# Sums of values four pieces to a visit, and planned steps that keep GpSimd's subtractions from VectorE's sums

## Chip, cores and metric

The kernel runs on one core of a Trainium2 chip. The metric is the device time of one execution in microseconds (us); lower is better. Before the change the median of three runs is 1843.38 us (1842.33 to 1844.65).

## What is computed

Agent attention over 4 batches of 12480 tokens of width 128 with 49 agents, and a two-layer network with a squared ReLU on its result. Cut to what matters:

```python
def sm(a, b):                                  # batches B = 4
    s = scale * (a @ b.transpose(0, 2, 1))     # scale = 1 / sqrt(128)
    s = s - s.max(-1, keepdims=True)
    e = np.exp(s)
    return e / (e.sum(-1, keepdims=True) + 1e-09)

a2k = sm(agents, k)          # 49 x 12480 for each batch
agent_v = a2k @ v            # 49 x 128
q2a = sm(q, agents)          # 12480 x 49
x = (q2a @ agent_v).reshape(49920, 128)
h = x @ w_in                 # 128 -> 2048
r = np.maximum(h, 0.0)
out = ((r * r) @ w_out).astype(np.float32)     # 2048 -> 128
```

All inputs are float32. The kernel splits both operands of each large product into a high and a low part and adds three products of the parts.

## The kernel before, in words

**The main loop.** The tokens are cut into 49 slabs of 1024. For each slab there are 16 steps (`NF`), for each tile of 512 tokens 8 steps (`NJ`), 784 in all. In step i, `mm1(i)` makes 256 hidden columns of one tile: six matmuls from the normalised query weights (`p_a`, `p_b`, high and low parts) and the folded weights `w_hi`, `w_lo`, which hold agent_v times w_in of the batch. ScalarE then takes the ReLU (`relu`), and for each two steps squares (`square`, 128x2048); VectorE makes the rounded high part `gh` (`high`, L453) and the low part `gl` (`low`, L457) of the square. `mm2` of step i works on the hidden columns of five steps earlier (`LAG`): twelve matmuls into one of two pairs of PSUM banks (`pair`), the last four from `gl`. After eight steps a tile is done; `store` adds the pair's two halves (ScalarE copy L482, VectorE sum `ob` L483) and sends the tile out.

**What is put between the steps.** TensorE, VectorE, ScalarE, GpSimd and the DMA queue of SyncE (SP) each execute their instructions in the order in which they are written out. That order comes from a list of (time in steps, function), which a planner fills and which is sorted at the end (`at`, `steps`). Every 16 steps the query path of one slab runs: for two slabs at a time `q_scores` on TensorE and `q_shift` on VectorE, then for each slab `q_exp` (ScalarE), `q_inverse` (VectorE), `q_norm` (GpSimd, L349), `q_hi` (ScalarE), `q_lo` (GpSimd, L362), a DMA transpose and sort, and the weave of two 16-bit planes (`q_weave`, half on ScalarE, half on GpSimd, L392), then `q_spread` by DMA into `p_a` and `p_b`.

**The next batch.** While batch b-1 is in the main loop, `plan_batch(b)` lays out the work on the keys and values of batch b = 1, 2, 3. Batch 0 is done ahead of the loop. The 12480 keys are 13 pieces of 960. First the key scores, two pieces to a visit of TensorE (`k_scores`, L179), with a copy to SBUF (`k_copy`) and a running maximum (`k_pmax`). When the maximum is known, each piece n gets `k_sub` (GpSimd, L214: the maximum is subtracted in place in `sk`), `k_exp` (ScalarE) and `e_sum` (VectorE, L232: the exponentials are added into `ea`). `v_acc` (TensorE, L229) multiplies the exponentials of some pieces with their values, 64 small matmuls a piece (128 records a visit of two pieces, as each fp32 matmul leaves two), in one visit between two steps of the main loop; `v_sum` (VectorE, L245, L247) adds its result to the sum of the batch. `v_load` fetches a piece of values into one of the nine buffers that key, query and value pieces and two stages of the query path share (`io`). At the batch's end `a_last` and `w_make_all` fold the result into `w_hi` and `w_lo`.

**The planner.** `chain(t, todo)` gives each operation of a list (engine, function, arguments) a whole step at or after t. `hop` holds the steps from one engine's operation to the next one's. A step that is in `taken` for an engine isn't given twice, with one exception: a VectorE operation that reads a bank directly behind its TensorE visit goes there all the same, and its step is put in `read`. Visits may only lie in steps in which the tile of `mm2` is at step 1, 3 or 5 (`slots`). The steps that carry a `store` are taken for ScalarE and VectorE (`ends`). The query path is planned first, then the batches. `low` has its place within a step by `read` and `ends`, so that moved visits move it by a fraction of a step. The planned steps set the order of instructions on each engine and nothing else: an engine executes its next instruction as soon as the inputs are there.

Of the kernel before, what the change touches and what calls it, by code (L numbers as in the profile page):

```python
# [25 lines left out]
def agent_attention_relu2_kernel(ctx: ExitStack, tc: tile.TileContext, qT, kT, v, agT, w_in, w_out, outT):  # L26
# [7 lines left out]
    B, NS = kT.shape[:2]  # L34
# [455 lines left out]
    def at(t, f, *args):  # L490
        steps.append((t, len(steps), f, args))
# [7 lines left out]
    slots = {i for i, m in second.items() if m % NJ in (1, 3, 5)}  # L499
    taken = {(e, i) for i in ends for e in ("ACT", "DVE")}  # L500
    read = set()

    def chain(t, todo):

        first = prev = None
        while todo:
            n = 1
            while todo[0][0] == "PE" and n < len(todo) and todo[n][1] in reads_bank and todo[n][0] != "PE":  # L510
                n += 1
            t += hop[prev][todo[0][0]] if prev else 0
            while True:
                g, p, ts = t, None, []
                for e, *_ in todo[:n]:
                    g += hop[p][e] if p else 0
                    while (e, g) in taken or (e == "PE" and g not in slots):
                        if p == "PE" and e == "DVE":
                            break
                        g += 1  # L520
                    ts.append(g)
                    p = e
                if todo[0][0] != "PE" or ts[-1] <= ts[0] + 1:
                    break
                t += 1
            for (e, f, *args), g in zip(todo, ts):
                soon = e == "DVE" and prev == "PE"
                if soon:
                    read.add(g)
                else:  # L530
                    taken.add((e, g))
                at(g + (.49 if soon and f is q_shift else .47 if soon else .45 if e == "PE" else .5), f, *args)
                prev = e
            first = ts[0] if first is None else first
            t, todo = ts[-1], todo[n:]
        return first, t
# [3 lines left out]
    def plan_tokens(s, base):  # L540
        todo = [("ACT", q_exp, s), ("DVE", q_inverse, s), ("POOL", q_norm, s), ("ACT", q_hi, s)]
        todo += [("POOL", q_lo, s)] + ([("PE", q_transpose, s), ("ACT", q_copy, s)] if s < 3 else [])
        if s > 1 and s % 2 == 0:
            m = min(2, NSG - s)
            first, base = chain(base, [("PE", q_scores, s, m), ("DVE", q_shift, s, m)])
            for x in range(s, s + m):
                at(first - 5, q_load, x)
            base += 3
        _, end = chain(base, todo)
        if s > 2:  # L550
            at(end + 2.4, q_turn, s)
            at(end + 4.9, q_sort, s)
            end += 8
            while any(("ACT", end + x) in taken for x in range(4)):
                end += 1
            _, end = chain(end, [("ACT", q_weave, s, 1, nc.scalar.copy)])
            taken.update(("ACT", end + x) for x in (1, 2))
            at(end + .6, q_weave, s, 0, nc.gpsimd.tensor_copy)
        at(max(end + 1.4, (s - 1) * NF + 9.9 if s % 2 else 0) if s > 2 else end + .9, q_spread, s)
        assert end + 3 < s * NF, (s, end)  # L560

    def plan_batch(b, base):

        end = b * N // TT * NJ
        for n in range(0, NS, 2):
            m = min(2, NS - n)
            first, t = chain(base + int(n * 4.6), [("PE", k_scores, b, n, m), ("ACT", k_copy, n, m), ("DVE", k_pmax, n, m)])
            for x in range(n, n + m):
                if b > 1 or x:
                    at(max(base - (6 if b > 1 else 0), first - 5), k_load, b, x)  # L570
            if n == NS - 3:
                chain(t + 1, [("DVE", k_max, 0, NS - 1)])
        _, t0 = chain(t + 1, [("DVE", k_max, 1)])
        _, t0 = chain(t0 + 4, [("PE", k_max, 2), ("DVE", k_max, 3)])
        _, t0 = chain(t0 + 3, [("PE", k_max, 4), ("DVE", k_max, 5)])
        done, d = {}, (end - 31 - t0) / NS
        for n in range(NS):
            _, done[n] = chain(t0 + 1 + int(n * d), [("POOL", k_sub, n), ("ACT", k_exp, n)])
            if n:
                _, y = chain(done[n] + 1, [("DVE", e_sum, n)])  # L580
            if n == NS - 1:
                _, y = chain(y + 1, [("DVE", a_last, 0)])
            if n % 2 or n == NS - 1:
                x = n - n % 2
                first, t = chain(done[n] + 2 if n % 2 else y + 4, [("PE", v_acc, x, n + 1 - x), ("DVE", v_sum, x)])
                for y in range(x, n + 1):
                    at(first - 5, v_load, b, y)
        at(first + .46, a_last, 1)
        at(t + .475, a_last, 2)
        _, e = chain(t + 2, [("PE", w_make_all, b, 0), ("ACT", w_make_all, b, 1), ("DVE", w_make_all, b, 2)])  # L590
        assert e + 2 < end, (e, end)
        return t + 1
# [30 lines left out]
    for n in range(NS):  # L623
        t = Z + 6.3 + 2.07 * n
# [43 lines left out]
    t = t0 + 13.4  # L668
# [22 lines left out]
    for y, x in enumerate((1.15, 1.16, 1.17)):  # L691
        at(x, w_first, 0, 4, 4, y, nc.vector)
    at(3.1, warm_rows, 6)
    plan_tokens(1, 3)
    for s in range(2, NSG):
        plan_tokens(s, (s - 2) * NF + (13 if s < 3 else 7 if s % 2 else 6))
    t = 0
    for b in range(1, B):
        t = plan_batch(b, t)
# [43 lines left out]
```

## Time and profile before

| | before |
|---|---|
| median of three runs | 1843.38 us |
| the profiled execution | 1842.06 us, its span 1840.3 us |
| TensorE busy | 1823.0 us, 99% |
| VectorE busy | 1689.1 us, 92% |
| ScalarE busy | 1676.8 us, 91% |
| GpSimd busy | 375.9 us, 20% |
| matmuls of the value visits (L229) | 2496 records in 21 visits |
| `k_sub` on GpSimd (L214) | 39 x 2238 ns |
| `e_sum` on VectorE (L232) | 33 x 879 ns and 3 x 1066 ns |

How to read it: the span runs from the first to the last instruction of the profiled execution; the rest of its time lies around it. Busy time is the sum of an engine's instructions. Matmuls overlap, so a busy TensorE isn't one at its peak; idle time in front of an instruction is shown with what ended it ("releaser").

### The profile page before, as it was taken

To read this page: it belongs to the slowest core of one execution; us is meant where nothing else is said; L and a number is where in the kernel's file an instruction comes from. 1 tells how busy PE (TensorE), PEld (TensorE's weight loads), DVE (VectorE), ACT (ScalarE), POOL (GpSimd) and SP (SyncE) were. 2 spreads that over 40 slices of the span, in tenths; PEclk is the share of its full clock that TensorE was granted. 3 is DMA by queue.
4 is the path that set the end of the run, shared out by engine and by line. 5 is a ranking of instruction groups with operands and counts; after the bars stand their busy time and mean duration, and the time that the engine had idled before them with its cause. 6 is when DMAs were issued, how large, how long until landed. Compare 5 with 4: busy or idle time off the path is not lost.

```text
span 1840.3 us, 51937 instructions
## 1 busy us (share of the span) xinstructions
PE 1823.0 (99%) x23244; PEld 1481.4 (80%) x23244; DVE 1689.1 (92%) x1274; ACT 1676.8 (91%) x1538; POOL 375.9 (20%) x199
## 2 busy tenths in 40 slices
PE   9899999999999999999999999999999999999999
PEld 8688888887888887878788788788878888888887
DVE  7789999999888999999988999999999999999997
ACT  5788999998989999999898999999999999999998
POOL 1111132222111222223111132132211112212110
PEclk9999999999999999999999999999999999999999
DMA  9334334434443334333434243324422322322320
GB/s 383 113 99 133 99 94 114 110 101 120 111 121 118 89 106 113 86 109 91 135 113 130 77 97 100 119 80 115 119 64 86 87 74 80 92 74 80 81 74 21
DMA packets 154514, 193.46 MB, mean 105 GB/s; under 512 B 102488, under 2 KB 102744, under 8 KB 154290
## 3 DMA queue, kind: packets, MB, share of 16 engines
q1 hardware_dynamic: 154290, 190.13, 35.5%
q8 instruction: 182, 2.98, 0.7%
q14 instruction: 42, 0.34, 0.1%
HBM read 83.02 MB, written 25.56 MB: 59 GB/s over the span
## 4 chain that ended last, share of the span: by engine, by line
PE 86%; ACT 5%; DVE 4%; issue 2%; DMA 1%; POOL 0%; SPq 0%; ACTq 0%; DVEq 0%; POOLq 0%
PE pair L477 53%; PE h L440 27%; PE pair L179 3%; ACT rg L446 3%; ACT rg L449 2%; PE pair L229 2%; DVE gl L457 2%; DVE gh L453 1%; DMA raw<-w_in 1%; PE pair L238 1%; DMA p_b<-w_lo 0%; PE pair L298 0%; POOL e L349 0%; ACT ob L482 0%; DVE e L334 0%
## 5 line engine op out<-in xcount | busy, mean ns | idle before, releaser
L457 DVE TENSOR_TENSOR gl<-rg,gh 128x2048 fp32r<-128x2048 f32 x391 | 937.6, 2398 | 18.6 <-DVE gh L453 0.9
L446 ACT ACTIVATE rg<-h 128x1024 f32<-128x1024 f32 (+1 forms) x784 | 790.9, 1020 | 118.7 <-PE h L440 116.6
L449 ACT ACTIVATE rg<-rg 128x2048 f32<-128x2048 f32 x391 | 748.7, 1915 | 7.3
L477 PE MATMUL pair<-gh,wo_hi 64*128 64x512 f32 x3136 | 632.3, 391 | 1.4 <-issue 1.4
L477 PE MATMUL pair<-gh,wo_lo 64*128 64x512 f32 x3136 | 633.4, 392 | 0.0
L453 DVE CAST gh<-rg 128x2048 fp32r<-128x2048 f32 x391 | 520.1, 1330 | 90.9 <-ACT rg L449 80.7
L477 PE MATMUL pair<-gl,wo_hi 64*128 64x512 f32 x3136 | 501.1, 391 | 4.0 <-DVE gl L457 3.1
L440 PE MATMUL h<-p_b,w_hi 49*128 49x512 f32 (+4 forms) x1616 | 503.2, 390 | 1.8 <-DMA p_b<-w_lo 1.8
L440 PE MATMUL h<-p_a,w_hi 49*128 49x512 f32 (+4 forms) x1616 | 498.3, 390 | 1.3 <-ACT rg L446 0.6
L477 PEld LDWEIGHTS pair<-gh,wo_lo 64*128 64x128 f32 x3136 | 314.6, 186 | 70.8 <-issue 2.2
L477 PEld LDWEIGHTS pair<-gh,wo_hi 64*128 64x128 f32 x3136 | 312.4, 185 | 66.7
L477 PEld LDWEIGHTS pair<-gl,wo_hi 64*128 64x128 f32 x3136 | 303.7, 184 | 72.0 <-DVE gl L457 5.4
L440 PEld LDWEIGHTS h<-p_a,w_hi 49*128 49x128 f32 x1616 | 287.6, 186 | 43.7 <-issue 3.2
L440 PEld LDWEIGHTS h<-p_b,w_hi 49*128 49x128 f32 x1616 | 290.9, 186 | 29.7 <-DMA p_b<-w_lo 2.4
L440 PE MATMUL h<-p_b,w_lo 49*128 49x512 f32 (+4 forms) x808 | 313.6, 388 | 0.0
L440 PE MATMUL h<-p_a,w_lo 49*128 49x512 f32 (+4 forms) x808 | 313.6, 388 | 0.0
L349 POOL TENSOR_TENSOR e<-e,sm 128x392 f32<-128x392 f32 x48 | 76.4, 1591 | 735.8 <-DVE sm L346 698.0
L392 POOL COPY woven<-planes 128x1024 uint16<-128x1024 uint16 x46 | 100.3, 2181 | 458.6 <-DMA planes<-turned 405.1
L440 PEld LDWEIGHTS h<-p_a,w_lo 49*128 49x128 f32 x808 | 148.4, 184 | 27.6
L440 PEld LDWEIGHTS h<-p_b,w_lo 49*128 49x128 f32 x808 | 148.4, 184 | 2.3
L362 POOL TENSOR_TENSOR pp<-e,pp 128x392 fp32r<-128x392 f32 x48 | 105.4, 2197 | 142.9 <-ACT pp L359 142.9
L214 POOL TENSOR_TENSOR sk<-sk,mM 120x392 f32<-120x392 f32 x39 | 87.2, 2238 | 15.6 <-DVE mM L211 15.6
(112 smaller groups left out, 854.8 us busy)
## 6 DMA issues: line engine op xcount, KB each, us to landing
vt<-v SPq DMA_DIRECT2D x52, 516.0 KB
qt<-qT SPq DMA_DIRECT2D x49, 512.0 KB
kt<-kT SPq DMA_DIRECT2D x52, 480.0 KB
outT<-ob SPq DMA_DIRECT2D x97, 256.0 KB
planes<-turned SPq DMA_DIRECT2D x184, 98.0 KB
p_a<-woven SPq DMA_DIRECT2D x92, 196.0 KB
p_b<-woven SPq DMA_DIRECT2D x92, 196.0 KB
raw<-w_in SPq DMA_DIRECT2D x4, 512.0 KB
```

The lines of the kernel that those rows point to most:

```text
L179: nc.tensor.matmul(ps[r, u, c * A:(c + 1) * A], x[:, c, r], ag_sb[:, batch(c, r), :], start=True, stop=True)
L214: eng.tensor_tensor(out=piece(n), in0=piece(n), in1=m.rearrange("p (o a) -> p o a", o=1).to_broadcast([CH, G, A]), op=ALU.subtract)
L229: nc.tensor.matmul(ps[r], vt[:CH, c, r], piece(x)[:, c, :], start=x == n and c == 0, stop=x == n + m - 1 and c == G - 1)
L349: eng.tensor_tensor(out=es[s], in0=es[s], in1=sms.pop(s).to_broadcast([P, G, A]), op=ALU.mult)
L362: eng.tensor_tensor(out=halves(s)[1], in0=es.pop(s), in1=halves(s)[0].bitcast(F32), op=ALU.subtract)
L392: copy(PT["x"][:, :, :, w], planes[:, w])
L440: nc.tensor.matmul(h[:, u, x0:x1], w[ra[u], j, :], pt[u ^ lo][ra[u], x0:x1], start=x == 0, stop=x == 2)
L446: nc.scalar.activation(rgs[p][:, x], hs.pop(i)[:, :, :width(i)], AF.Relu)
L449: nc.scalar.activation(rgs[p], rgs[p], AF.Square)
L453: nc.vector.tensor_copy(ghs[p], rgs[p])
L457: nc.vector.tensor_tensor(out=gls[p], in0=rgs.pop(p), in1=ghs[p].bitcast(F32), op=ALU.subtract)
L477: nc.tensor.matmul(outs[t][u][:, :width(i)], w[rg[u], 2 * j + e, :], g[rg[u], e, :], start=j == 0 and x == 0, stop=j == NJ - 1 and x == 5)
```

## The change

Five edits of the planner. No function that computes is changed.

- `apart` and the condition in `chain`: a `k_sub` isn't planned in a step, or one before a step, that is taken for VectorE; an `e_sum` isn't planned in a step, or one after a step, that is taken for GpSimd.
- Two steps behind the start of a `q_scores` visit, TensorE's step is taken, so that no visit of a batch lies there.
- ScalarE's two steps ahead of a weave are taken, and GpSimd's two steps from the weave on.
- `v_acc` takes four pieces to a visit in place of two, so that a batch has visits of 4, 4, 4 and 1 pieces in place of six of 2 and one of 1; `v_sum` follows each.
- Of the loads of a visit's values, the first two are placed nine steps ahead of the visit, the others five, as all were before.

```diff
@@ -500,6 +500,9 @@
     taken = {(e, i) for i in ends for e in ("ACT", "DVE")}
     read = set()
 
+    def apart(e, f):
+        return (("DVE", 0), ("DVE", 1)) if e == "POOL" and f is k_sub else (("POOL", 0), ("POOL", -1)) if f is e_sum else ()
+
     def chain(t, todo):
 
 
@@ -512,9 +515,9 @@
             t += hop[prev][todo[0][0]] if prev else 0
             while True:
                 g, p, ts = t, None, []
-                for e, *_ in todo[:n]:
+                for e, f, *_ in todo[:n]:
                     g += hop[p][e] if p else 0
-                    while (e, g) in taken or (e == "PE" and g not in slots):
+                    while (e, g) in taken or (e == "PE" and g not in slots) or any((x, g + z) in taken for x, z in apart(e, f)):
                         if p == "PE" and e == "DVE":
                             break
                         g += 1
@@ -543,6 +546,7 @@
         if s > 1 and s % 2 == 0:
             m = min(2, NSG - s)
             first, base = chain(base, [("PE", q_scores, s, m), ("DVE", q_shift, s, m)])
+            taken.add(("PE", first + 2))
             for x in range(s, s + m):
                 at(first - 5, q_load, x)
             base += 3
@@ -553,8 +557,10 @@
             end += 8
             while any(("ACT", end + x) in taken for x in range(4)):
                 end += 1
+            taken.update(("ACT", end - x) for x in (1, 2))
             _, end = chain(end, [("ACT", q_weave, s, 1, nc.scalar.copy)])
             taken.update(("ACT", end + x) for x in (1, 2))
+            taken.update(("POOL", end + x) for x in (0, 1))
             at(end + .6, q_weave, s, 0, nc.gpsimd.tensor_copy)
         at(max(end + 1.4, (s - 1) * NF + 9.9 if s % 2 else 0) if s > 2 else end + .9, q_spread, s)
         assert end + 3 < s * NF, (s, end)
@@ -580,11 +586,11 @@
                 _, y = chain(done[n] + 1, [("DVE", e_sum, n)])
             if n == NS - 1:
                 _, y = chain(y + 1, [("DVE", a_last, 0)])
-            if n % 2 or n == NS - 1:
-                x = n - n % 2
-                first, t = chain(done[n] + 2 if n % 2 else y + 4, [("PE", v_acc, x, n + 1 - x), ("DVE", v_sum, x)])
+            if n % 4 == 3 or n == NS - 1:
+                x = n - n % 4
+                first, t = chain(done[n] + 2 if n < NS - 1 else y + 4, [("PE", v_acc, x, n + 1 - x), ("DVE", v_sum, x)])
                 for y in range(x, n + 1):
-                    at(first - 5, v_load, b, y)
+                    at(first - (5 if y > x + 1 or n == x else 9), v_load, b, y)
         at(first + .46, a_last, 1)
         at(t + .475, a_last, 2)
         _, e = chain(t + 2, [("PE", w_make_all, b, 0), ("ACT", w_make_all, b, 1), ("DVE", w_make_all, b, 2)])
```

## Rows read from the trace of the kernel before

**Rows 1.** The page's busy times, share of the span and instructions of each engine.

```profile
PE 1823.0 (99%) x23244; PEld 1481.4 (80%) x23244; DVE 1689.1 (92%) x1274; ACT 1676.8 (91%) x1538; POOL 375.9 (20%) x199
```

**Rows 2.** The page's chain that ended last, its shares by engine.

```profile
PE 86%; ACT 5%; DVE 4%; issue 2%; DMA 1%; POOL 0%; SPq 0%; ACTq 0%; DVEq 0%; POOLq 0%
```

**Rows 3.** Timeline of TensorE, steps round a value visit: start, us, engine, line, operation, [idle].

```profile
312.89 0.62 PE L440 MATMUL h<-p_b,w_hi 49*128 49x512 f32 x2
...
315.08 1.62 PE L229 MATMUL pair<-sk,vt 120*32 120x49 f32 x128
...
318.83 0.39 PE L440 MATMUL h<-p_b,w_hi 49*128 49x512 f32 x1
```

**Rows 4.** Timeline of TensorE, steps round a one-piece visit of key scores.

```profile
190.74 0.62 PE L440 MATMUL h<-p_a,w_hi 49*128 49x512 f32 x2
...
195.95 0.39 PE L440 MATMUL h<-p_a,w_hi 49*128 49x512 f32 x1
```

**Rows 5.** View of line 229: what the engine, and who for it, waited for: us, times.

```profile
  DVE ob L483: 3.0, 7
  DVE e L334: 1.9, 4
...
  DVE a L247: 0.3, 1
```

**Rows 6.** Timeline of TensorE at the three places where it stands for gl.

```profile
720.51 0.62 PE L440 MATMUL h<-p_b,w_hi 49*128 49x512 f32 x2
...
722.61 0.62 PE L440 MATMUL h<-p_b,w_hi 49*128 49x512 f32 x2
...
725.15 0.73 PE L477 MATMUL pair<-gl,wo_hi 64*128 64x512 f32 x4 [0.75 <-DVE gl L457]
...
725.72 0.63 PE L440 MATMUL h<-p_b,w_hi 49*128 49x512 f32 x2
...
798.89 0.73 PE L477 MATMUL pair<-gl,wo_hi 64*128 64x512 f32 x4 [0.58 <-DVE gl L457]
...
1170.78 0.73 PE L477 MATMUL pair<-gl,wo_hi 64*128 64x512 f32 x4 [0.56 <-DVE gl L457]
```

**Rows 7.** Timeline of VectorE ahead of the first of these places.

```profile
716.24 2.75 DVE L457 TENSOR_TENSOR gl<-rg,gh 128x2048 fp32r<-128x2048 f32 x1
718.91 1.32 DVE L232 TENSOR_TENSOR ea<-sk,ea 120x392 f32<-120x392 f32 x1
720.16 1.98 DVE L453 CAST gh<-rg 128x2048 fp32r<-128x2048 f32 x1
```

**Rows 8.** Groups by line: the sums of exponentials, busy us, mean ns | idle before.

```profile
L232 DVE TENSOR_TENSOR ea<-sk,ea 120x392 f32<-120x392 f32 x33 | 29.0, 879 | 0.0
```

**Rows 9.** Views of lines 232, 457, 453: duration ns min/median/max, first and last start.

```profile
L232 DVE TENSOR_TENSOR ea<-sk,ea x33: 551/560/1667, 260.9 to 1327.0; 120x392 f32<-120x392 f32 x33
...
L457 DVE TENSOR_TENSOR gl<-rg,gh x391: 1220/2293/3434, 64.1 to 1832.7; 128x2048 fp32r<-128x2048 f32 x194, 128x1024 fp32r<-128x1024 f32 x2
...
L453 DVE CAST gh<-rg x391: 685/1227/2382, 62.8 to 1832.0; 128x2048 fp32r<-128x2048 f32 x194, 128x1024 fp32r<-128x1024 f32 x2
```

**Rows 10.** Timeline of GpSimd over the same stretch as rows 7.

```profile
717.48 2.33 POOL L362 TENSOR_TENSOR pp<-e,pp 128x392 fp32r<-128x392 f32 x1 [0.64 <-ACT pp L359]
719.76 3.19 POOL L214 TENSOR_TENSOR sk<-sk,mM 120x392 f32<-120x392 f32 x2
```

**Rows 11.** Busy us (instructions) of PE, PEld, DVE, ACT, POOL by stretch; clock, DMA share, GB/s.

```profile
246.00:426.00 180.00, 179.80 (x2446) 144.70 (x2444) 173.00 (x125) 167.54 (x156) 50.56 (x25) 1.00 0.37 104
384.00:421.00 37.00, 37.00 (x322) 29.79 (x320) 35.36 (x25) 36.40 (x36) 13.57 (x7) 1.00 0.32 91
1687.00:1749.00 62.00, 62.00 (x536) 49.95 (x534) 58.45 (x41) 60.33 (x55) 12.87 (x6) 1.00 0.25 67
```

**Rows 12.** Timeline of TensorE at two stalls whose end no view explains.

```profile
526.59 0.40 PE L477 MATMUL pair<-gh,wo_hi 64*128 64x512 f32 x1 [1.38 <-issue]
...
1099.04 0.72 PE L477 MATMUL pair<-gl,wo_hi 64*128 64x512 f32 x3 [0.93 <-issue]
```

## The prediction

> **What bounds the kernel now.** I read the page's busy times first, then the chain that ended last, then TensorE's timeline of single steps. TensorE (PE) is busy 99% of the span, VectorE (DVE) 92%, ScalarE (ACT) 91%, GpSimd (POOL) 20% [rows 1]; 86% of the chain lies on PE [rows 2]. So the time is PE's work plus PE's stalls. One step of the loop (six first-layer matmuls, twelve second-layer) takes 2.10 us where nothing else happens: the steps that start at 720.51 and 722.61 in [rows 6] are that far apart, and 784 x 2.10 = 1646 us. What the change can touch is the remainder: the small matmuls put between the steps ("visits") and the places where PE waits. VectorE is next: in batch 1's value phase it is busy 173.0 of 180 us, and ScalarE 167.5 [rows 11]. A change that moves their work about can make PE wait, so I look for gains in PE rows and for dangers in DVE rows.
>
> **What a visit costs, and what fusing saves.** The two steps around a two-piece value visit take 318.83 - 312.89 = 5.94 us against 4.20, so the visit adds 1.74 us [rows 3]. Two steps around a one-piece visit (key scores, the same 64 matmuls a piece) take 195.95 - 190.74 = 5.21, so it adds 1.01 [rows 4]. A piece therefore costs 0.73 us and a visit 0.28 us besides: the wait for the first weights and the slower first matmuls behind it. The pieces stay, 39 in three batches. Visits go from 7 a batch (six of two, one of one) to 4 (three of four, one of one): 9 fewer. Sure gain: 9 x 0.28 = **2.5 us** on PE, all of it on the path that sets the end.
>
> A visit also waits now and then for VectorE to have read the bank that it will use: its loads and matmuls stood 3.0 us for the output sum (7 times) and 1.9 us for the query shift (4 times), in 21 visits [rows 5]. Nine fewer visits of 21 would take 9/21 x 4.9 = 2.1 us of that, were it all PE time; loads run ahead of matmuls, so the lower bound is nothing. I take **0.8 us**, nearer the lower end, because most of the 0.3 to 0.6 us of such a wait lies under the matmuls still running. The nine sums on VectorE that go (0.2 us each by the neighbours) are hidden by PE and count nothing.
>
> **What the separation of steps saves.** PE stands for `gl`, VectorE's low half, at three places: idle 0.75, 0.58 and 0.56 us [rows 6]. The first step takes 725.72 - 722.61 = 3.11 us, 1.01 over the plain 2.10, so 0.26 is lost beside the idle time; with the same 0.26 the three cost 1.01 + 0.84 + 0.82 = **2.7 us**. The first place on VectorE: `gl` 2.75, then `ea` (the sum of exponentials, `e_sum`) 1.32, then `gh` 1.98 [rows 7], against medians of 2.29, 0.56 and 1.23 [rows 9]. That is 0.46 + 0.76 + 0.75 = 1.97 us of lengthening in one run, while GpSimd executes `q_lo` (2.33) and two `k_sub` (3.19) back to back [rows 10]. The same order (`q_lo`, then `k_sub`, with `e_sum` between) precedes the other two. Under the new rule no `e_sum` is planned in the step of a GpSimd operation or the one after; stepping the planner's rules through both texts gives 19 of 36 so placed before and none after. At 282 to 286, where PE stood for 1.01 us, `e_sum` moves from step 282 to 286, past `q_lo` and the `k_sub` that follows it. Its 1.32 us then lies behind the late `gl` in place of ahead of it, which is more than the 1.01 us that was missing. So I count the 2.7 us as gone.
>
> Not all collisions go. The 33 sums of the common form average 879 ns against a median of 560 [rows 8, 9]: 33 x 0.319 = 10.5 us, at 0.76 each about 14 lengthened. GpSimd does not follow its planned steps: the two `k_sub` of [rows 10] are planned eight steps (17 us) apart and run back to back, since its queue holds an operation only until its inputs are there, and theirs have long been. So a `k_sub` planned away from `e_sum` still starts right behind the `q_norm`, `q_lo` or weave ahead of it. Laying the 36 new `e_sum` steps beside such times, I find about 5 that still meet one. Three stalls belong to some 15 collisions; 5 would keep a third, **0.9 us** (bounds 0 and 2.7).
>
> A rule speaks against this half. The row first: beside GpSimd, `gl` is 0.46 and `gh` 0.75 longer too [rows 7, 9], so a subtraction moved away from `e_sum` meets one of these. The Trainium skill ("SBUF — State Buffer", Who interferes with whom) says that a VectorE instruction with two SBUF inputs, or in a two-port mode, contends with a GpSimd one that reads SBUF, and that the first to issue blocks the other for its whole length. By that rule the lengthening is only passed on; the trace agrees in kind, though 0.46 us is not the whole of any GpSimd instruction. That result is rival 1.
>
> **The other edits.** The loads of values: the last two of each four go out 5 steps (10.5 us) ahead, the first two 9; before, both 5. They pass the query path's transposes, sorts and spreads in SP's queue. The DMA engines are at 37% in batch 1's value phase [rows 11], the nine-buffer ring still gives every tile 7 steps or more between release and reuse by the plan, and a spread that waits for 1 MB ahead of it (some 5 us) is planned at least 6 steps before its slab: nothing; without that cover each late one would cost up to its 5 us. The reserved PE slot two steps behind `q_scores` pushes key-score visits later by 2 to 10 steps; their count and work are the same: nothing. The ACT steps reserved ahead of a weave only move `k_exp`: nothing; bounds for both, -1 to +1 us, one stall of the size of [rows 6]. A new wait: VectorE's `v_sum` must wait for a visit longer by 2 x 0.73 = 1.46 us, and `low` is queued behind it. PE is itself inside that visit then, so nobody asks for `gl` sooner; the two-piece visits made `v_sum` wait once, for 0.3 us [rows 5]. Nothing.
>
> Two stalls of PE show no cause but "issue" (1.38 us, and a second of 0.93) [rows 12]. I can't tell whether a shifted order keeps, loses or adds such: 0, with bounds of -2.3 and +2.3.
>
> **Sum.** -2.5 - 0.8 - 2.7 + 0.9 = -5.1 us. The profiled execution took 1842.06 us (span 1840.3); it becomes 1837.0. It lies 1.3 us below the median of the three runs, 1843.38, so I expect **1838.3 us**, 0.28% less. What this kernel's measurement can tell from no change is about 0.2%, 3.7 us, so the line between faster and same is 1839.7.
>
> **Rivals.** *1. The steps are separate in the plan alone.* GpSimd runs ahead and the lengthening falls on `gl` and `gh`, so that as many stalls come up elsewhere: only the fusing counts, -2.5 - 0.8 = -3.3, 1840.1 us, the same. For it: [rows 10]. Against: at the three stalls it was the sum itself, 1.32 us, that stood between two lengthened instructions.
>
> *2. The long stretch starves PE (slower).* A visit lets VectorE and ScalarE catch up. Four-piece visits land 6 to 8 steps ahead of a query visit in eight cases, and leave eight stretches of 24 to 26 steps with none; the longest before was 20. In 24 steps PE needs 50.4 us, plus 1.7 for the query visit. VectorE needs 12 x (1.23 + 2.29) = 42.2 [rows 9], nine GpSimd operations at about 0.6 each 5.4, three sums 1.7, three output sums 2.0, two query inverses 1.9 and a shift with its maximum 1.9: 55.1 us, 3.0 too many. The lag of five steps carries part. If half came through in all eight, 8 x 1.5 = 12 us less the 6.0 gained would be +6.0: 1849.4 us. The gain is used up from 0.75 us a stretch, and it is slower beyond measurement from 1.2. Against it: 37 us without any visit have PE busy 37.00 with VectorE at 35.36, and 62 us of the last phase, with no value work, 62.00 of 62 [rows 11]; instructions overlap at their ends, so that the sum above is too high. A mild form, 0.5 us a stretch, gives -6.0 + 4.0 = -2.0: 1841.4 us, the same.
>
> *3. More than I count.* No collision stalls PE and the bank waits give their 2.1 us: -2.5 - 2.1 - 2.7 = -7.3, 1836.1 us.
>
> **How the numbers follow.** Forecast 0.40, rival 1 0.30, rival 3 0.14, rival 2 mild 0.06 and full 0.10. Faster by over 0.2%: 0.40 + 0.14 = 0.54; within 0.2%: 0.36; slower: 0.10. The range runs from 1835.0 (rival 3 with half of the "issue" stalls gone) to 1845.0 (a mild rival 2 with both bounds of "issue" and the moved visits against me, 1844.7); it leaves out rival 2's full price.
>
> **What the profile of the changed kernel would show.** Right: 12 value visits in place of 21, a four-piece one adding 0.28 + 4 x 0.73 = 3.2 us; `e_sum` near 0.6 us on average; no PE idle for `gl` in the value phases; GpSimd's busy time hardly changed. Wrong, rival 1: `e_sum` short, `gl` and `gh` longer on average, and waits for `gl` at new places. Wrong, rival 2: waits for `gl` or for ScalarE's `rg` gathered late in the stretches ahead of the four-piece visits. Should the visit's own cost of 0.28 not show nine times, the first term is wrong.

## The result, and the profile after

The changed kernel takes 1867.8 us (median of four runs, 1865.63 to 1870.73), the kernel before 1843.85 us (four runs beside them, 1842.33 to 1844.65): the ratio is 1.0132, 95% interval 1.0114 to 1.0149. It is slower by 24 us, and outside the predicted range of 1835 to 1845. The profiled execution of after took 1865.63 us with a span of 1863.9 us; against the profiled execution of before that is 23.6 us more. One run of those below, of the two-piece version, took 2205.08 us at a granted clock of 0.752; it is a slow one, and the range given there leaves it out.

The page's busy times and chain of after, which answer to [rows 1, 2]:

```profile
PE 1827.7 (98%) x23244; PEld 1492.3 (80%) x23244; DVE 1680.5 (90%) x1265; ACT 1674.7 (90%) x1538; POOL 383.4 (21%) x199
...
PE 95%; DVE 2%; issue 2%; ACT 1%; DVEq 0%
```

No other engine took over: VectorE is busy 8.6 us less, ScalarE 2.1 us less, and PE has more of the chain than before. PE has as many matmuls as before and is busy only 4.7 us longer. So most of the loss, 18.9 of the 23.6 us, is idle time of PE. The view of waits (what PE stood for, us in total, times, longest) says how it is labelled:

```profile
PE pair L229 <- issue: 17.4, 8, 2.9
PE pair L179 <- issue: 5.1, 2, 4.5
PE pair L238 <- DMA vt<-v: 1.8, 1, 1.8
PE pair L477 <- DVE gl L457: 1.5, 2, 1.1
...
PE pair L477 <- issue: 1.0, 2, 0.5
```

"Issue" is a wait for nothing that the profile shows. Before, PE stood so twice, both times at L477 [rows 12]; now it does eight times inside the value visits (L229) and twice inside visits of scores (L179); two short stands at L477 come to 1.0 us. The two waits for `gl` lie ahead of 75 us; the three of [rows 6] are gone. The same in a budget, from TensorE's timeline: what each kind of step takes beyond the plain 2.10 us, summed (a step is counted from one last matmul of `mm2` to the next; the last four steps, which are shorter, are left out).

```
                                  before            after
18 two-piece value visits         34.4 us           -
 9 four-piece value visits        -                 52.9 us (4.25 to 8.34 each)
 3 one-piece value visits          4.0               3.4
41 two-piece visits of scores     72.6              81.9 (one of them 8.19)
 7 further visits of L179, L298   10.3              10.3
 8 other small visits              4.0               3.0
   steps without a visit           5.3               2.5
   sum                           130.5             153.9
```

The sum differs by 23.4 us, nearly the whole of the 23.6. The nine fused visits cost 18.5 us more than the eighteen they replace, and one visit of key scores 6.4 us more. The steps without a visit give 2.8 us back: the three waits for `gl` of [rows 6] (2.7 us) and the first stall of [rows 12] (1.8) are gone from them, and smaller losses at other places, the largest 0.8 in a step behind a stop, take part of it again.

How a four-piece visit looks, in TensorE's timeline (start, us, engine, line, operation, count, [idle]); it answers to [rows 3]:

```profile
278.48 0.64 PE L440 MATMUL h<-p_b,w_hi 49*128 49x512 f32 x2
...
280.69 2.70 PE L229 MATMUL pair<-sk,vt 120*32 120x49 f32 x208
285.15 0.74 PE L229 MATMUL pair<-sk,vt 120*32 120x49 f32 x48 [1.75 <-issue]
285.82 0.73 PE L440 MATMUL h<-p_b,w_hi 49*128 49x512 f32 x2
...
289.31 0.62 PE L440 MATMUL h<-p_a,w_hi 49*128 49x512 f32 x1
...
1179.21 2.57 PE L229 MATMUL pair<-sk,vt 120*32 120x49 f32 x210
1184.63 1.20 PE L229 MATMUL pair<-sk,vt 120*32 120x49 f32 x46 [2.85 <-issue]
```

PE does 208 of the 256 matmuls at full pace, stops for 1.75 us in the middle of an unbroken run of one kind of matmul whose inputs are all there, and does the other 48. Behind the stop the matmuls come slowly. The windows before and over this visit (busy us of PE, PEld, DVE, ACT, POOL; clock, DMA share, GB/s):

```profile
270.00:279.00 9.00, 9.00 (x82) 7.14 (x80) 8.74 (x6) 8.83 (x10) 8.38 (x4) 1.00 0.64 193
279.00:286.00 7.00, 5.25 (x274) 4.45 (x272) 4.90 (x5) 3.09 (x3) 1.18 (x1) 1.00 0.48 129
```

and of PE alone, the 4 us behind this stop and behind four others (PE busy; clock, DMA share, GB/s):

```profile
286.00:290.00 4.00, 4.00 (x22) 0.57 0.46 171
...
804.00:808.00 4.00, 4.00 (x38) 1.00 0.49 136
...
948.00:952.00 4.00, 4.00 (x20) 0.50 0.04 15
1185.00:1189.00 4.00, 4.00 (x57) 0.50 0.40 113
1267.00:1271.00 4.00, 4.00 (x52) 1.00 0.51 188
```

At three of ten stops the granted clock went from 1.00 to 0.50 or 0.57 (the lower of its two levels, 1.2 GHz in place of 2.4, for most or all of the window), and the 22 instructions of the first such window are about half of the 38 in a plain one. The stop was 2.0, 4.8 and 3.1 us long there, but 3.1 and 2.3 us at two where the clock stayed. So the loss of the nine visits can be split. They add 52.9 us, and 9 x 3.2 = 28.8 was foretold: 24.1 too many. The gaps in the list below make 20.3 of that, and the two visits with the slow clock 3.3 beyond their gaps (1.22 and 2.04).

### The profile page after: what moved, and what is told of

Read it like the earlier page. It is cut to its first block, busy times and chain, and to the rows that moved or that the text cites. A ratio compares the mean times of both kernels' runs of the same rounds, so it can differ in the third digit from the quotient of the medians.

```text
span 1863.9 us, 51915 instructions
## 1 busy us (share of the span) xinstructions
PE 1827.7 (98%) x23244; PEld 1492.3 (80%) x23244; DVE 1680.5 (90%) x1265; ACT 1674.7 (90%) x1538; POOL 383.4 (21%) x199
## 3 DMA queue, kind: packets, MB, share of 16 engines
q8 instruction: 182, 2.98, 0.7%
## 4 chain that ended last, share of the span: by engine, by line
PE 95%; DVE 2%; issue 2%; ACT 1%; DVEq 0%
PE pair L477 58%; PE h L440 30%; PE pair L179 4%; PE pair L229 2%; PE pair L612 1%; DVE sk L214 0%; PE pair L298 0%; DVE gl L457 0%; DVE pm L194 0%; PE pair L238 0%; DVE cv L109 0%; ACT rg L449 0%; DVE gh L453 0%; DVE cv L110 0%; PE h L179 0%
## 5 line engine op out<-in xcount | busy, mean ns | idle before, releaser
L477 PE MATMUL pair<-gh,wo_lo 64*128 64x512 f32 x3136 | 638.8, 393 | 0.4 <-issue 0.4
L477 PE MATMUL pair<-gh,wo_hi 64*128 64x512 f32 x3136 | 637.6, 392 | 0.4 <-DVE gh L453 0.4
L477 PE MATMUL pair<-gl,wo_hi 64*128 64x512 f32 x3136 | 505.1, 392 | 2.1 <-DVE gl L457 1.5
L477 PEld LDWEIGHTS pair<-gh,wo_lo 64*128 64x128 f32 x3136 | 318.9, 186 | 68.0 <-issue 0.3
L477 PEld LDWEIGHTS pair<-gh,wo_hi 64*128 64x128 f32 x3136 | 316.7, 185 | 67.5 <-issue 1.0
L477 PEld LDWEIGHTS pair<-gl,wo_hi 64*128 64x128 f32 x3136 | 306.6, 185 | 69.4 <-DVE gl L457 4.0
L392 POOL COPY woven<-planes 128x1024 uint16<-128x1024 uint16 x46 | 90.8, 1973 | 424.8 <-DMA planes<-turned 363.6
L440 PEld LDWEIGHTS h<-p_a,w_lo 49*128 49x128 f32 x808 | 148.9, 184 | 25.8 <-DVE w_lo L290 0.5
L214 POOL TENSOR_TENSOR sk<-sk,mM 120x392 f32<-120x392 f32 x39 | 102.5, 2631 | 1.3 <-DVE mM L211 1.3
```

The costliest lines, as they stand in the source:

```text
L214: eng.tensor_tensor(out=piece(n), in0=piece(n), in1=m.rearrange("p (o a) -> p o a", o=1).to_broadcast([CH, G, A]), op=ALU.subtract)
L392: copy(PT["x"][:, :, :, w], planes[:, w])
L440: nc.tensor.matmul(h[:, u, x0:x1], w[ra[u], j, :], pt[u ^ lo][ra[u], x0:x1], start=x == 0, stop=x == 2)
L477: nc.tensor.matmul(outs[t][u][:, :width(i)], w[rg[u], 2 * j + e, :], g[rg[u], e, :], start=j == 0 and x == 0, stop=j == NJ - 1 and x == 5)
```

## What the stops are

The page of after has a queue that the prediction passed over (packets, MB, share of 16 engines):

```profile
q8 instruction: 182, 2.98, 0.7%
```

The page of before has the same line. 2.98 MB / 182 is 16 KB a packet; PE has 2 x 23244 instructions (a weight load and a multiply for each matmul), and 46488 / 182 is 255. So this queue seems to bring PE's own instructions, in blocks of 256. I numbered PE's instructions in the order in which they ran (two for each matmul and one for each recorded wait), and looked up the place at which it resumes. The gap is that between two weight loads; "transfer" is how long before the resumption the last packet of q8 began.

```
after:  visit at   stops behind matmul   gap us   resumes at place   transfer us before
         280.69        208 of 256         2.00      193 of 256         2.33
         356.62        none inside        0.94      194, in the step behind it   2.77
         434.31*       205                1.99      193                2.34
         710.50*       180                2.50      193                3.26
         803.20*       226                3.13      193                2.38
         877.28*       160                2.39      193                2.29
        1179.21        210                3.10      194                2.36
        1266.80*       236                2.33      194                2.39
        1340.41*       171                1.90      193                2.24
         941.22 (key scores) 121 of 128   4.76      194                2.45
before:  526.59*  (L477)                  2.01      194                2.42
        1099.04*  (L477)                  1.54      193                2.28
                                    (* time of the resumption)
```

Every stop ends at the same place of the count, 193 or 194 modulo 256, and so do the two stalls of before that I had to leave without a cause [rows 12]. Two shorter stops of after, 0.83 us at 161.70 and 1.05 at 925.27, end there as well. Over the whole run PE passes place 193 of the count 182 times, once for each packet of the queue. Each resumption comes 2.2 to 3.3 us after a block's transfer began. So PE seems to have run out of instructions. The sizes fit. A piece is 32 matmuls in the kernel's text, each of which leaves two records: 64 in the trace. These 64, in 0.73 us, are 128 instructions, so a block of 256 lasts 15 us in plain steps (36 instructions in 2.1 us) and 1.46 us in a visit. A two-piece visit is 256 instructions and passes the border of a block once. A four-piece visit is 512 and passes it twice within 1.46 us, and the second block isn't there: from one border to the first instruction behind the next it took 1.46 us plus a gap of 1.9 to 3.1.

I call this theory S (supply). The rivals: L, the long visit itself or the work beside it stops PE (banks, VectorE, the loads 9 steps ahead); P, the changed planning does (separation, reserved steps).

## The experiments

**One part of the change undone or done alone.** The first run keeps every edit but the fused visits:

```diff
-            if n % 4 == 3 or n == NS - 1:
-                x = n - n % 4
+            if n % 2 or n == NS - 1:
+                x = n - n % 2
...
-                    at(first - (5 if y > x + 1 or n == x else 9), v_load, b, y)
+                    at(first - 5, v_load, b, y)
```

> The changed kernel with two pieces to a value visit again and all loads of values 5 steps ahead; the other edits of the planner (subtractions and sums in separate steps, reserved steps) stay. Theory S (supply): TensorE's instructions arrive in blocks of 256; a four-piece visit has 512 and runs dry inside, so without fusing no value visit idles over 0.5 us and the time is 1838 to 1846 us (one stall of a key-score visit at a block's end, up to 6 us, may stay). Theory P (plan): the moved order costs the time, so it stays at 1860 or more. Theory L (length): the long visit starves ScalarE and VectorE or lets TensorE's clock fall by its small matmuls alone; 1838 to 1846 as for S.

Measured: 1835.87 us (ten runs, 1832.39 to 1842.40), ratio to before 0.9958 (0.9941 to 0.9975), below the expected 1838 to 1846. It beats both kernels. TensorE's waits in its profiled execution:

```profile
PE pair L179 <- issue: 4.9, 2, 4.4
PE pair L477 <- DVE gl L457: 1.5, 2, 1.1
```

No value visit stops; the eighteen add 1.73 to 1.88 us each, 31.9 in all against 34.4 before. The key-score visit still does. The second run is the complement, the kernel before with the fused visits and their loads alone:

> The kernel before with nothing but the four-piece visits and their loads (9 and 5 steps ahead); none of the rules on separate or reserved steps. Theory S: 9 four-piece visits of 512 instructions; at least 7 of them idle for 1.8 us or more, behind matmul 128 of 256 at the earliest, and the time is 1860 to 1870 us. Theory P: without the moved order 1840 to 1846. Theory L: 1860 to 1870, but idle time follows no place in the instruction stream.

Measured: 1873.74 us (1864.65 to 1878.89), ratio 1.0161 (1.0116 to 1.0207), above the expected 1860 to 1870. TensorE's waits:

```profile
PE pair L229 <- issue: 19.2, 9, 2.8
PE pair L477 <- DVE gl L457: 5.0, 8, 1.2
```

All nine visits stop, at place 193 or 194, and the waits for `gl` are there. P falls: fusing alone costs the time. The third is the kernel before with the separation rule (`apart`) alone:

> The kernel before with nothing but the rule that keeps subtractions and sums in separate steps; no reserved steps, visits of two pieces, loads as before. If the three waits for gl near steps 287, 319 and 479 came from the sum between two lengthened instructions, none of these three is left and the sum averages under 0.7 us; 1838 to 1842 us. If the lengthening only moves on (rival 1 of the prediction): waits for gl of the same total elsewhere, 1842 to 1845.

Measured: 1839.83 us (1837.94 to 1843.06) against 1842.11 beside it, ratio 0.9987 (0.9978 to 0.9996). TensorE's waits:

```profile
PE pair L477 <- issue: 2.6, 2, 1.7
...
PE pair L477 <- DVE gl L457: 0.9, 2, 0.5
```

The three stands for `gl` of [rows 6] are gone (before: 3.1 us in 5 waits; the two that are left lie ahead of 75 us in both), and the time is 2.3 us less. The mean sum is 752 ns, where under 0.7 us was expected.

**Half the instructions, the same long visit.** This tells S from L. The value matmuls of the changed kernel write 64 columns in place of 32, so a four-piece visit is 256 instructions and not 512; pieces, loads, banks and the plan stay.

```diff
-                for r in rv:
+                for r in rg:
```

> The changed kernel with value matmuls 64 columns wide in place of 32: half as many instructions, so that a four-piece visit has 256 in place of 512; same steps, loads, pieces. A one-piece group of 32 such matmuls takes about 0.9 us in batch 0's key scores against 0.73 for 64 narrow ones, so a visit itself gets 0.6 to 0.8 us longer. Theory S: no idle time over 1 us inside a value visit, step with a visit 6.0 to 6.5 us in place of 7.2 to 10.4, total 1845 to 1854 us. Theory P and theory L: visits are as long or longer, so the stalls stay and the total is 1866 or more.

Measured: 1842.03 us (1840.64 to 1844.99), 25.8 us less than after and below the expected 1845 to 1854; ratio to before 0.9990 (0.9978 to 1.0002). TensorE's timeline of the first four-piece visit, and the queue's line on the page:

```profile
276.91 0.62 PE L440 MATMUL h<-p_b,w_hi 49*128 49x512 f32 x2
...
279.11 3.94 PE L229 MATMUL pair<-sk,vt 120*64 120x49 f32 x128
282.98 0.72 PE L440 MATMUL h<-p_b,w_hi 49*128 49x512 f32 x2
```

```profile
q8 instruction: 172, 2.82, 0.6%
```

The visit is 3.94 us long, longer than the 3.2 that was predicted of the narrow one, and has no stop; all nine steps with such a visit take 6.16 or 6.17 us. L falls: a visit of four pieces, with the same bank, buffers and neighbours, runs through once it is 256 instructions and not 512. And the queue follows PE's count: with 2 x 21996 instructions PE passes place 193 of the count 172 times, and the queue has 172 packets.

**A size between.** Three pieces a visit (`n % 3 == 2`) are 384 instructions: a border is passed once or twice, by where the visit begins.

> The changed kernel with three pieces to a visit (visits of 3, 3, 3, 3, 1 a batch): 384 instructions. Theory S: a visit runs dry only if fewer than 128 instructions of the current block are left when it starts, so about half of the 12 three-piece visits (4 to 8) idle for 1.5 us or more, each behind matmul 128 at the earliest and at one and the same place in blocks of 256 instructions; total 1850 to 1862 us. Theory L: all 12 lose something, in proportion to their length. Theory P: 1860 or more.

Measured: 1847.24 us (1843.21 to 1855.96), ratio 1.0024 (1.0005 to 1.0044), better than I expected. Four of the twelve three-piece visits are lengthened (steps of 6.34 to 8.29 us), all four with the resumption at place 193 or 194; the other eight take 4.54 to 4.82 us. The undisturbed 4.55 is 2.45 over the plain step: 0.28 + 3 x 0.72. So the prediction's price of a visit was right wherever the instructions were there.

**The place moved.** If the place in the stream sets the stop, 64 more instructions at the very start move each stop 32 matmuls ahead in its visit. The run is the changed kernel plus 32 tiny matmuls whose result isn't used:

```diff
+    def shift(n):
+        for _ in range(n):
+            nc.tensor.matmul(pairs[0][rg[0], 0, :2], warm[:, :L], warm[:, :2], start=True, stop=True)
+
+    at(Z, shift, 32)
```

> The changed kernel with 32 tiny matmuls more at the very start (64 instructions, ahead of the first data), so that every later instruction lies a quarter of a block further on. Theory S: in each four-piece visit the idle time comes 32 matmuls earlier than in the changed kernel, where it came behind matmul 208, none, 205, 180, 226, 160, 210, 236, 171: so near 176, 229, 173, 148, 194, 128, 178, 204, 139, and all at the same place in blocks of 256 as before. Theory L: at the same matmuls as in the changed kernel, or without order. Time 1862 to 1874 either way.

Measured: 1859.87 us in one run (1862 to 1874 expected). TensorE's timeline, first two four-piece visits:

```profile
277.96 2.30 PE L229 MATMUL pair<-sk,vt 120*32 120x49 f32 x176
282.31 1.09 PE L229 MATMUL pair<-sk,vt 120*32 120x49 f32 x80 [2.06 <-issue]
...
352.59 3.12 PE L229 MATMUL pair<-sk,vt 120*32 120x49 f32 x238
357.98 0.43 PE L229 MATMUL pair<-sk,vt 120*32 120x49 f32 x18 [2.27 <-issue]
```

The first visit stops behind matmul 176 where it stopped behind 208: exactly 32 earlier. The second, which had run through, now stops behind 238 (expected 229). Over the nine: 176, 238, 173, 148, 194, just behind the visit, 178, 204 and none, against the expected 176, 229, 173, 148, 194, 128, 178, 204 and 139. Six fall on the very matmul, one nine beside it; all stops seen end at 193 or 194. Two were expected and not seen inside a visit: whether a block comes in time at a border also depends on when its transfer begins, which the count alone doesn't give.

**What was left: one key-score visit.** In after and in the first two-piece run the key-score visit planned at step 376 stops though it passes one border only; the block's transfer began 4.8 and 4.9 us after PE passed the border ahead of it, and 0.95 MB of data moved in that time. First its keys were loaded four steps earlier (`first - 9` in place of `first - 5`):

> e1_two with the loads of the keys of batches 2 and 3 nine steps ahead of their visit in place of five; the order of TensorE's instructions is the same. Theory S with late blocks by data traffic: in e1_two two key loads of 480 KB go out 1.6 us ahead of the visit at step 376, the fetch of instructions starts only 2 us after TensorE has run dry, and the visit adds 8.1 us. With the loads 8 us earlier the fetch finds the DMA engines free: that visit adds under 4.0 us, total 1833 to 1837 us. Theory B (the fetch is late whatever the data traffic, by the block's border alone): it still adds over 6 us in the profiled execution.

Measured: 1838.49 us (1835.31 to 1842.15), ratio 0.9980 (0.9970 to 0.9990). The stop stays (3.77 us behind matmul 118, the transfer 4.2 us after the border). This doesn't clear the data: the keys' loads went out at 921.96 us in place of 925.17, ahead of the weights' transfers in place of behind them, and that is still less than 5 us ahead of the border. Then the transfers of the weights (`q_spread`) were planned away from that border, and in another run onto two borders ahead of other visits:

> The two-piece version with one edit: the four transfers of slab 24's weights (q_spread, 784 KB) go out four steps (8.4 us) later, at planned step 378.4 in place of 374.4, behind the key-score visit planned at step 376. In the two-piece version TensorE passed the place where it asks for its next block of instructions at 925.31 us, the transfers had gone out from 921.75 on, the block's transfer began only at 930.24, 4.9 us after, and TensorE stood 4.35 us inside that visit. Theory (data transfers in flight delay the block of instructions): the block's transfer begins about 1 us after the pass, the visit adds 1.7 to 1.9 us in place of 8.1, and the median falls to the lower group of the two-piece version's runs, 1832 to 1835 us, with a spread of less than 5 us between its runs (10 there). Rival (the late transfer has to do with the place in the stream or the keys' loads, and not with these transfers): the visit still adds 7 us or more and the runs scatter from 1832 to 1842.

> The two-piece version with the opposite edit: the transfers of slabs 7 and 11 (q_spread) go out 3.5 steps (7.3 us) earlier, at planned steps 102.4 and 166.4 in place of 105.9 and 169.9, so that they begin some 3.5 us ahead of the passes at 293.14 and 437.93 us, each about 4 us ahead of a key or query visit (steps 103 and 167, which added 1.79 and 1.87 us undisturbed). Theory (data transfers in flight delay the block of instructions): at both visits the block's transfer begins 3 to 5 us after the pass and TensorE stands 1 to 4 us in the visit or right behind it, at place 193 or 194 of 256; the run comes to 1835 to 1848 us, 2 to 8 us more than without. Rival: both visits stay at 1.7 to 1.9 us.

Measured: 1837.50 us (1832.95 to 1843.60) and 1834.12 us in one run. Neither decides, because neither edit moved the transfers as planned: SP's queue stands at the `store` ahead of them until its `ob` is there, and they went out at 920.99 us (first at 921.75) and at 295.60 and 441.53 us (first at 297.08 and 441.64). A planned time between two stores sets an order and no time. But they show something else. In the first of them the keys' loads and the weights' transfers went out in the same order and at the same distance from the border as with the early key loads (4.6 us ahead of it in both), and the block's transfer began 0.2 us after the border where it was 4.2 there. TensorE's timeline of the key-score visit in the second, which has the same instructions and the same order ahead of this visit as the two-piece version:

```profile
925.90 1.50 PE L179 MATMUL pair<-ag_sb,kt 128*32 128x49 f32 x118
927.63 0.35 PE L179 MATMUL pair<-ag_sb,kt 128*24 128x49 f32 x10 [0.23 <-issue]
```

and in the two-piece version's first profile:

```profile
926.80 1.50 PE L179 MATMUL pair<-ag_sb,kt 128*32 128x49 f32 x118
932.65 0.52 PE L179 MATMUL pair<-ag_sb,kt 128*24 128x49 f32 x10 [4.35 <-issue]
```

PE stops behind the same matmul, once for 4.35 us and once for 0.23. The transfer began 4.9 us after the border in the one and 0.9 in the other. The place is fixed by the stream; how late the block is changes from execution to execution.

Last, the two-piece version with 56 tiny matmuls ahead (112 instructions), beside itself again:

> The two-piece version with 56 tiny matmuls (112 instructions, 2 columns each, result not used) ahead of everything, some 0.4 us of work, so that every later instruction lies 112 places further in its block of 256. At the key-score visit planned at step 376, the place 193/194 that ended 1.5 us ahead of the visit is then passed some 6 us earlier (112 instructions at 36 in 2.1 us), and the next lies behind the visit. Theory (place in the stream): that visit adds 1.7 to 1.9 us in every profile, and the median is 1832 to 1835 us unless another visit now has a border in its way (an interval between two borders of 1.85 us at 131 and of 1.93 at 1178 us would be the likeliest; then up to 3 us more). Rival (the visit itself, its keys or its transfers make the stall): 7 us or more added there, and runs from 1832 to 1842 as before.

> The two-piece version again, unchanged, beside the shifted one on the same chip. Theory (the stall at the key-score visit comes and goes between executions): runs from 1832 to 1843 us, median 1834 to 1839, 1 to 5 us above the shifted version. Rival: the two do not differ.

Measured: 1835.59 us (1834.45 to 1836.94), ratio 0.9957 (0.9944 to 0.9970), and 1834.21 us (1832.98 to 1834.63), ratio 0.9950 (0.9935 to 0.9964). Shifted, the key-score visit runs through (step of 3.81 us), and small stops came up at other places (at 813.51 us, 0.49; at 964.98, 0.66), again at place 193 or 194. But the unshifted version had no stop there either this time, and is no slower. So the shift has no gain to show, and that the stop at this visit makes the two-piece version scatter is not shown.

**The reserved step.** The two-piece version without the reserved TensorE step behind `q_scores`:

> e1_two (two pieces to a visit, all other edits) without the TensorE step reserved behind the query scores; key-score visits of batches 2 and 3 then lie 0 to 10 steps earlier (174 for 176, 216 for 222, 224 for 234 in batch 2). Theory S (supply), with which the 4.6 us idle of a key-score visit in e1_two's profiled execution is a block of instructions that came late: the blocks' borders fall elsewhere in the key phase, so that visit's stall may go and another may come; 1834 to 1841 us. Theory A (the reserved step is what makes e1_two faster than before): 1841 to 1845.

Measured: 1846.11 us (1836.99 to 1849.35), ratio 1.0013 (0.9998 to 1.0028). That is above both ranges, and in the median the two-piece version's gain over before is gone, as theory A has it. The profiled execution is one of the quick ones (1838.96) and shows a stall of before again (resumption at 526.26, place 193). What line 229 waited for (us, times), here and in the profile of the unshifted two-piece version (1832.98):

```profile
  DVE e L334: 7.7, 8
  issue: 5.1, 14
```

```profile
  issue: 5.5, 15
  DVE gl L457: 1.5, 4
```

Without the reserved step the loads and matmuls of the value visits stand 7.7 us, in eight waits, for VectorE's shift of the query scores (L334), and with it never. In the budget the value visits (of two pieces and of one) add 39.0 us against 35.3, the three small visits of L204 1.2 against 0.3, and the steps without a visit, with the stall, 2.0 more. What the slower executions lose beyond that isn't in a profile; that stays open.

## Why the prediction was wrong, step by step

**The failed step is the price of a four-piece visit**: "a four-piece one adding 0.28 + 4 x 0.73 = 3.2 us". It added 4.25 to 8.34, 5.88 on average: nine visits cost 52.9 us in place of 28.8. I took the cost of a piece from visits of one and two [rows 3, 4], that is of 128 and 256 instructions, and drew the line on to 512, past the size of the block that both had been within. As arithmetic on durations it was right (the undisturbed visits of the three-piece version confirm both 0.28 and 0.72); the resource that ends between the two sizes was not in my list. None of the rivals was this one: rival 2 looked for a slow case in VectorE and ScalarE, which did not come.

**The second failed step is the zero for "issue".** I wrote that I couldn't tell whether a shifted order keeps, loses or adds such stalls, with bounds of 2.3 us. The two stalls of [rows 12] were the only showing of this limit in the trace of before, and I bounded the term by their sum, not by what they could become. Two rows of before would have told more: the instruction queue on its page (182 packets of 16 KB there too, for 46488 instructions), and a run of 256 instructions in 1.62 us [rows 3], which is a block in less time than the 2.4 us (2.42 and 2.28) by which the transfer led the resumption at the two stalls. The Trainium skill ("Runtime: NRT & Kernel Launch", Instruction fetch mechanics) does name the blocks of 256 instructions and calls the cost of crossing one mostly hidden. In plain steps the runs agree (a block lasts 15 us). In the visits they don't: 1.9 to 3.1 us at each second border, and there the measurement decides.

**The three waits for `gl`, -2.7: right.** Separation alone gave -2.3 us of time, and neither there nor in after does PE stand for `gl` behind 75 us. That the steps without a visit take 2.8 us less in after is no second measurement of it: the first stall of [rows 12] went from them too.

**What remains of the collisions, +0.9: the count was about right, the cost was nothing.** I counted about 5 sums still lengthened, and priced a third of the stalls to them; no wait for `gl` is left in the value phases. The groups by line of after (busy us, mean ns), which answer to [rows 8]:

```profile
L457 DVE TENSOR_TENSOR gl<-rg,gh 128x2048 fp32r<-128x2048 f32 x391 | 933.2, 2387 | 19.0 <-DVE gh L453 0.5
L453 DVE CAST gh<-rg 128x2048 fp32r<-128x2048 f32 x391 | 522.6, 1337 | 94.4 <-ACT rg L449 87.7 <-PE pair L477 5.0 <-PE h L440 0.2
...
L232 DVE TENSOR_TENSOR ea<-sk,ea 120x392 f32<-120x392 f32 x33 | 22.9, 694 | 0.0
```

and on GpSimd, in both kernels, after first:

```profile
L214 POOL TENSOR_TENSOR sk<-sk,mM 120x392 f32<-120x392 f32 x39 | 102.5, 2631 | 1.3 <-DVE mM L211 1.3
```

```profile
L214 POOL TENSOR_TENSOR sk<-sk,mM 120x392 f32<-120x392 f32 x39 | 87.2, 2238 | 15.6 <-DVE mM L211 15.6
```

The mean sum is 694 ns; over the undisturbed 559 that is 33 x 0.135 = 4.5 us, at 0.76 each about 6 sums. Rival 1's mechanism is not borne out on VectorE: `gl` and `gh` together take 1455.8 us against 1457.7. The lengthening went to the other side. The subtractions take 15.3 us more on GpSimd, and what waits for them is what waited before (ScalarE, 2.3 us in 4 times).

**The bank waits, -0.8: the size was near, the reason wrong.** In after PE's loads wait 0.4 us for `ob` where it was 3.0 [rows 5]. But with the fused visits alone the loads and matmuls still wait 2.7 us, in 6 waits, and with two-piece visits and all the planning edits they don't wait for `ob` at all. There the eighteen visits come down from 34.4 to 31.9 us; 1.4 of that is the second stall of [rows 12], which lay in one of them, so about 1.1 is left for the banks. It was the moved visits that did this, not their number.

**The other edits at nothing, -1 to +1: not borne out, in the kernel's favour.** The two-piece version, with separation and the reserved steps and without fusing, is 0.4 to 0.5% faster than before in its two comparisons, 7.7 and 9.2 us; separation is 2.3 of these. So 5.4 to 6.9 us come from edits that I had put at zero, and without the reserved TensorE step the median shows no gain any more. I had looked at the number and the work of the visits that this step moves, which stay the same, and not at the bank that a visit just behind `q_scores` has to wait for. What the reserved steps of ScalarE and GpSimd are worth by themselves no run shows.

## What to carry to other kernels

Before a stretch of small instructions is made longer, count its instructions against the block in which the engine gets them, here 256, and compare the time that a block lasts with the time that the next one needs; a price taken from stretches within a block doesn't carry past one. A stall that a profile calls "issue" in the middle of uniform work is to be numbered: if all such stalls end at one place modulo 256, the engine ran out of instructions, and fewer, larger instructions or a break with ordinary work between two runs mend it. A planned time sets an order only, so an edit that is to move a transfer is to be looked up in the queue's timeline first.

## What the runs showed of the hardware

- TensorE's instructions come by DMA in blocks of 256 (16 KB, 0.9 to 1.7 us a transfer at the stops listed), and at a stop PE resumes 2.2 to 3.3 us after the transfer begins. PE's passings of a block's border and the queue's packets are equal in number, 182 and 182, and 172 and 172 with the wide matmuls. At 5.7 ns an instruction a block lasts 1.46 us; two borders within that time stopped PE for 1.9 to 3.1 us in eight of the nine four-piece visits of after, and just behind the ninth.
- From the border to the start of the next block's transfer is not constant: 0.2 to 0.9 us in some executions and 4.2 to 4.9 us in others at the same visit of nearly the same program. In the two-piece version's first profile the transfer began 2.7 to 2.9 us after the border in the median of the 13 borders behind which data moved at more than 300 GB/s for 2 us (six of them ahead of the main loop), and in the median no more than 0.5 us after it where it was under 200 GB/s. That is a relation between rows and no experiment; what delays them is open.
- The granted clock fell in or behind three of the ten stops in after (of 2.0, 3.1 and 4.8 us) and stayed at 1.00 behind others of the same length (2.0, 2.5 and 3.1). Where it fell, PE had 20 and 22 matmuls of plain steps in windows of 4 us in place of 38. What tells the two apart isn't in these rows.
